# Fillers, the place of the ranking and the gather, and the last batch's first layer, in an mLSTM cell followed by a mixture of depths

## The chip, the core and the metric

The kernel runs on one core of a Trainium2 chip. The metric is the device time of one execution in microseconds, the median of several. Five engines work side by side, each through its own instructions in order: TensorE (PE; its weight loads are listed apart as PEld), VectorE (DVE), ScalarE (ACT), GpSimd (POOL) and SyncE (SP), which here only issues transfers. They wait for each other through semaphores. Matmul results go to PSUM[...]; everything else lies in SBUF.

## The reference

Two blocks follow one another. The first is an mLSTM cell over 4 batches, 8 heads, 768 steps and head dimension 40:

```python
for t in range(S):
    m_new = np.maximum(f_gate[:, :, t] + m, i_gate[:, :, t])
    f_stab = np.exp(f_gate[:, :, t] + m - m_new)
    i_stab = np.exp(i_gate[:, :, t] - m_new)
    m = m_new
    C = f_stab[..., None, None] * C + i_stab[..., None, None] * np.einsum('bhd,bhe->bhde', vt, kt)
    n = f_stab[..., None] * n + i_stab[..., None] * kt
    h_tilde = np.einsum('bhde,bhe->bhd', C, qt)
    denom = np.maximum(np.abs(np.einsum('bhd,bhd->bh', n, qt)[:, :, None]), 1.0)
    y[:, :, t] = sigmoid(o_gate[:, :, t]) * h_tilde / denom
```

Its output, seen as x of shape (4, 768, 320), goes to a mixture of depths:

```python
scores = np.einsum('bsd,d->bs', x, w_gate)
out = x.copy()
for b in range(B):
    top_idx = np.argpartition(-scores[b], capacity)[:capacity]   # capacity 128
    xe = x[b, top_idx]
    ye = np.maximum(xe @ w1, 0.0) @ w2                           # 320 -> 1024 -> 320
    out[b, top_idx] = x[b, top_idx] + sigmoid(scores[b, top_idx])[:, None] * ye
```

## The kernel before

Each batch of 768 rows is cut into six chunks of 128, so there are 24 steps n, with b = n // 6 and c = n % 6. Within a chunk the recurrence is a masked product: W is exp of a difference of two gate sums, one 128 x 128 block for each head, made by matmuls of prepared "operands" (a_o and M_o) into PSUM (pW) and an exp on ScalarE; GpSimd zeroes its upper part (`causal`). T holds k and q transposed, pS the products of k and q, P the product of pS and W, pH the chunk's own numerator and denominator. What comes from earlier chunks is the state C, decayed on GpSimd (`decay`) and enlarged by a product of k and wv, where wv is v scaled by `cols`; `exchange` makes both products in pIC.

```python
def warm(n):
    pw = ps_c.tile([128, 4 * L], FP, name="pw", tag="c")
    for _ in range(n):
        nc.tensor.matmul(pw, fill[:, 0:128], fill, start=True, stop=True)
...
def columns(g):                     # chunks 3g to 3g + 2: three transposes
    pc = ps_m.tile([128, 3, NR], FP, name="pc", tag="m")
    for j, row in enumerate((wk[g], r[g], r[g][:, L - 1:L].to_broadcast([NR, L]))):
        nc.tensor.transpose(pc[:, j, :], row, ident[0:NR, 0:NR])
    return pc

def keep(g, pc):                    # and their copy to SBUF
    both = const.tile([128, 3, NR], FP, name=f"cols{g}")
    nc.vector.tensor_copy(out=both, in_=pc)
...
def turned(n):                      # T[n]: four transposes and a copy, for k and for q
    T[n] = work.tile([128, 2, NP, L], FP, name="T")
    for j in range(2):
        turn(loaded[n][0], j, T[n])
```

Once a batch's six chunks are there, its rows are ranked by comparing every score with every other: `spread` puts a chunk's scores along the free dimension (sb), `compare` counts (ge, cnt), `columns_of` sums the counts over the chunks in PSUM (pcol), `ranked` turns them into ranks and one-hot selections. `number` makes row numbers of these by matmuls (pidx), and `gather` fetches the 128 rows from what has been stored, by an indirect transfer that GpSimd issues. The two layers of batch b are then spread over the steps of batch b + 1. The middle of a step, with the parts of the one-time steps 7 and 8 (NT is 6):

```python
pH = within(P[n], v1)
if n == NT + 1:
    pcol = columns_of(state[0][1][2])
elif n == NT + 2:
    picked[0] = gather(0, number(sel[0], token))
elif n == NT + 3:
    enter(0)
soon = c == 0 or n == N - 1
if n + 1 < N:
    decay(*steps[n + 1])
    hide(n + 1)                                    # causal, if not done yet
    give = exchange(*steps[n + 1], loaded[n + 1][0], T[n + 1], wv[n + 1])
    if n + 1 not in pS:
        pS[n + 1] = products(T[n + 1])
...
num, sor = norm(nums.get(n), pH, so)
if n + 1 < N:
    nums[n + 1] = exchanged(*steps[n + 1], *give)
    if n + 1 not in P:
        P[n + 1] = weighted(pS[n + 1], W[n + 1])
...
if n == NT + 1:
    ranked(0, pcol)
if n + 2 < N:
    stated(n + 2)                                  # wv
...
if c > 0:
    result(b, c, num, sor)                         # x, and its store
score(b, c, state[b][0])
```

The last batch has no steps after it, so its selection, its two layers and the scatter of its rows stand at the end. Its selected rows are made on chip, by matmuls of x and the selection (pX), already transposed; the last 64 of the 320 features fill only half the partitions, and the rest is zeroed:

```python
w = HW[-1][1]                                      # 64
if w < 128:
    nc.gpsimd.memset(last.xeT[w:, NDC - 1], 0.0)
...
for j, (d0, w) in enumerate(HW):
    for t in range(NT):
        nc.tensor.matmul(pX[j][0:w], x_t[b, t][:, d0:d0 + w], sel[:, t], start=(t == 0), stop=(t == NT - 1))
    if j < 2:
        copies[j](out=last.xeT[0:w, j], in_=pX[j][0:w])
...
copies[2](out=last.xeT[0:w, 2], in_=pX[2][0:w])
last.idx, last.xe = gather(b, number(sel_h, token))
last.first(0, NFC)                                 # 24 matmuls of 128x128x128, two copies with relu
last.gate()
last.gated()
last.second(0, NFC)                                # 8 matmuls of 128x128x320
last.leave()                                       # ye, and the scatter
```

The profile counts each float32 matmul as two, so `first` is 48 records and `second` 16.

Of the kernel before, what the change touches and what calls it, by code (L numbers as in the profile page):

```python
# [21 lines left out]
def kernel(  # L22
# [40 lines left out]
    assert S == NT * L and NT == 6 and D < DP and H == 8 and B == 4 and NFC == 8 and F_ == NFC * 128  # L63
# [27 lines left out]
    fill = const.tile([128, 4 * L], BF, name="fill")  # L91
# [91 lines left out]
    def warm(n):  # L183

        pw = ps_c.tile([128, 4 * L], FP, name="pw", tag="c")
        for _ in range(n):
            nc.tensor.matmul(pw, fill[:, 0:128], fill, start=True, stop=True)  # L187
# [108 lines left out]
    def load_w1(j):  # L296
        d0, w = HW[j]
        nc.sync.dma_start(out=w1[0:w, j, :], in_=moe_w1[d0:d0 + w, :])
# [204 lines left out]
    class Layers:  # L503
# [34 lines left out]

        def second(self, f0, f1):
            if f0 == 0:  # L540
                self.py = ps_m.tile([K_, DM], FP, name="py", tag="m")
            for f in range(f0, f1):
                nc.tensor.matmul(self.py, self.hT[:, f, :], w2[:, f, :], start=(f == 0), stop=(f == NFC - 1))  # L543
# [62 lines left out]
    def hide(n):  # L606
        if n not in hidden:
            causal(W[n])
            hidden.add(n)

    def run(hooks):
        for f in hooks:
            f()

    def step(n, **more):
# [5 lines left out]
        if n == NT + 1:  # L621
            pcol = columns_of(state[0][1][2])
        elif n == NT + 2:
            picked[0] = gather(0, number(sel[0], token))
        elif n == NT + 3:
            enter(0)

        soon = c == 0 or n == N - 1
        if n + 1 < N:
            decay(*steps[n + 1])  # L630
            hide(n + 1)
            give = exchange(*steps[n + 1], loaded[n + 1][0], T[n + 1], wv[n + 1])
# [16 lines left out]
        if n == NT + 1:  # L649
            ranked(0, pcol)  # L650
# [3 lines left out]
        if n < NT + 3:  # L654

            turned(n + 2)
            run(more.get("spread", ()))
# [22 lines left out]
        if c > 0:  # L680
            result(b, c, num, sor)
# [21 lines left out]
    warm(9)  # L703
# [7 lines left out]
    pW = masked([(ps_h, "h"), (ps_c, "c")])  # L711
    split(0, 0, nc.vector, slice(0, BH))
# [59 lines left out]
    turned(3)  # L772
    pH = within(P[1], loaded[1][1])
# [25 lines left out]
    step(2, places=[second_places], spread=[lambda: spread(0, *state[0][1][:2])],  # L799
         end=[lambda: compare(0, *state[0][1])])  # L800
    for n in range(3, N):
# [18 lines left out]
        if n == NT + 1 and HW[-1][1] < 128:  # L820
            nc.gpsimd.memset(w1[HW[-1][1]:, NDC - 1, :], 0.0)
# [34 lines left out]
    w = HW[-1][1]  # L856
    if w < 128:
        nc.gpsimd.memset(last.xeT[w:, NDC - 1], 0.0)
# [3 lines left out]
    pX = [(ps_s, "s"), (ps_s, "s"), (ps_t, "t")]  # L862
    pX = [pool.tile([128, K_], FP, name=f"pX{j}", tag=tag) for j, (pool, tag) in enumerate(pX)]
    for j, (d0, w) in enumerate(HW):
        for t in range(NT):
            nc.tensor.matmul(pX[j][0:w], x_t[b, t][:, d0:d0 + w], sel[:, t], start=(t == 0), stop=(t == NT - 1))
        if j < 2:
            copies[j](out=last.xeT[0:w, j], in_=pX[j][0:w])
# [36 lines left out]
```

## Time and profile before

| what | value |
|---|---|
| device time, median of 3 | 187.53 us (187.52 to 190.49) |
| device time of the profiled execution | 193.54 us |
| its span, first to last instruction | 191.8 us |
| PE, PEld, DVE, ACT, POOL busy | 179.0, 149.8, 139.8, 99.9, 101.4 us |
| transfers | 24.37 MB, 127 GB/s on average |
| costliest group on POOL | the masks of W, 46 of 718 ns, 32.0 us |
| costliest group on DVE | P, 48 of 685 ns, 30.9 us |
| costliest groups on PE | pS 29.7, pt 28.2, pH 28.1, ph 23.8 us |

The page of a profile gives for each group of instructions its line, engine, operation, the tiles it writes and reads, how many there are and how long one takes, and then the idle time of the engine just before them and what ended most of it. The chain follows the execution back from its last instruction, at each step to what released it. The timeline lists instructions by start; a bracket at its end is the idle time before, with the releaser. "(x319)" is a number of instructions. Matmuls overlap, so a busy PE need not be PE at its peak.

### The profile page before, as it was taken

The numbers are of one execution on the slowest core, as the hardware profiler recorded it, in microseconds if no ns is written. First come the engines' busy times: TensorE is split into PE (matmuls) and PEld (weight loads), VectorE is DVE, ScalarE is ACT, GpSimd is POOL, SyncE is SP. The second block draws the span as 40 slices with busy tenths as digits, with TensorE's granted clock in tenths as the row PEclk, the third lists the DMA queues.
The fourth block names the chain that finished last, engine by engine and source line by source line (L and its number), as shares of the span: only waits on it lengthen the run. The fifth ranks groups of instructions, "written<-read, shape, count | busy, mean of one in ns | idle before, by whom it ended". The sixth has DMA issues, their size and how long they took to land.

```text
span 191.8 us, 6510 instructions
## 1 busy us (share of the span) xinstructions
PE 179.0 (93%) x2594; PEld 149.8 (78%) x2594; DVE 139.8 (73%) x413; ACT 99.9 (52%) x233; POOL 101.4 (53%) x171
## 2 busy tenths in 40 slices
PE   6999999789999887999999999999999999989990
PEld 2577888677877775989878889798788898859960
DVE  7633748988999868867899778868997788585101
ACT  3054466589898678466734473567344734201110
POOL 7954356597676639413774657327746571023202
PEclk9999999999999999999999999999999999999999
DMA  4999996597998999999999498597993101010100
GB/s 79 140 156 148 145 171 100 108 173 151 198 223 180 164 224 251 170 172 183 159 172 143 98 166 152 104 188 120 147 127 83 39 34 38 36 38 36 34 0 34
DMA packets 105854, 24.37 MB, mean 127 GB/s; under 512 B 100640, under 2 KB 105248, under 8 KB 105824
## 3 DMA queue, kind: packets, MB, share of 16 engines
q1 hardware_dynamic: 105008, 22.50, 74.0%
q0 software_dynamic: 384, 1.31, 2.2%
q8 instruction: 20, 0.33, 0.8%
q10 hardware_dynamic: 432, 0.15, 0.7%
q14 instruction: 10, 0.08, 0.2%
HBM read 19.37 MB, written 4.59 MB: 125 GB/s over the span
## 4 chain that ended last, share of the span: by engine, by line
PE 65%; issue 11%; DVE 11%; POOL 7%; DMA 3%; ACT 1%; POOLq 1%; ACTq 0%
PE pS L363 11%; PE pH L420 10%; PE pt L308 10%; PE ph L534 9%; PE py L543 5%; PE pIC L389 4%; PE pIC L395 4%; PE pW L341 3%; DVE P L369 3%; POOL W L347 3%; PE pw L187 2%; DMA out_dram<-ye,idx 2%; DMA xe<-out_dram,idx 2%; DVE ge L459 1%; POOL sor L435 1%
## 5 line engine op out<-in xcount | busy, mean ns | idle before, releaser
L342 ACT ACTIVATE W<-pW 128x512 f32<-128x512 f32 x48 | 26.1, 595 | 24.6 <-PE pW L341 15.2
L435 POOL TENSOR_TENSOR sor<-so,rec 128x320 f32<-128x320 f32 x24 | 17.8, 740 | 39.1 <-DVE rec L433 32.8
L347 POOL TENSOR_SCALAR_AFFINE_SELECT W<-W 128x512 f32<-128x512 f32 x46 | 32.0, 718 | 10.9 <-ACT W L342 10.9
L369 DVE TENSOR_TENSOR P<-pS,W 128x512 f32<-128x512 f32 x48 | 30.9, 685 | 7.6 <-PE pS L363 3.7
L309 ACT COPY T<-pt 128x512 f32<-128x512 f32 x47 | 25.5, 589 | 20.0 <-PE pt L308 19.7
L420 PEld LDWEIGHTS pH<-v,P 128*64 128x64 f32 x768 | 24.9, 140 | 9.8 <-DVE x L440 5.5
L420 PE MATMUL pH<-v,P 128*64 128x64 f32 x768 | 28.1, 227 | 3.8 <-DVE x L440 2.4
L363 PE MATMUL pS<-T 64*128 64x128 f32 x384 | 29.7, 297 | 0.0
L308 PE MATMUL pt<-ident,qk 128*128 128x128 f32 x192 | 28.2, 294 | 0.0
L363 PEld LDWEIGHTS pS<-T 64*128 64x128 f32 x384 | 24.9, 199 | 2.5 <-issue 1.3
L459 DVE SCALAR_TENSOR_TENSOR ge<-sb,sc,earlier 128x128 bf16<-128x128 f32 (+5 forms) x23 | 17.5, 764 | 11.0 <-ACT sb L453 10.9
L308 PEld LDWEIGHTS pt<-ident,qk 128*128 128x128 f32 x192 | 23.3, 151 | 1.5 <-issue 0.2
L534 PE MATMUL ph<-xeT,w 128*128 128x128 f32 x192 | 23.8, 280 | 0.0
L534 PEld LDWEIGHTS ph<-xeT,w 128*128 128x128 f32 x192 | 22.1, 192 | 1.7 <-issue 1.6
L543 PE MATMUL py<-w,hT 128*128 128x320 f32 x64 | 19.3, 442 | 0.0
L354 POOL TENSOR_TENSOR wv<-v,cols 128x328 f32<-128x328 f32 x20 | 15.1, 756 | 5.4 <-DVE cols L284 5.4
L446 DVE CUSTOM_DVE_ANT_0 scr<-x,wg 128x320 f32<-128x320 f32 x24 | 15.7, 652 | 0.7
L543 PEld LDWEIGHTS py<-w,hT 128*128 128x128 f32 x64 | 11.5, 191 | 5.0 <-issue 1.4
L389 PE MATMUL pIC<-C,T 128*64 128x82 f32 x320 | 15.2, 236 | 0.0
L549 POOL DMA_INDIRECT out_dram<-ye,idx x4 | 4.6, 1144 | 19.4 <-DVE ye L547 19.4
L395 PE MATMUL pIC<-wv,qk 128*64 128x41 f32 x320 | 12.8, 230 | 0.7 <-POOL wv L354 0.7
L377 POOL TENSOR_TENSOR C<-C,cols 128x328 f32<-128x328 f32 x16 | 13.0, 810 | 0.2
(150 smaller groups left out, 265.4 us busy)
## 6 DMA issues: line engine op xcount, KB each, us to landing
qk<-in_k_dram SPq DMA_DIRECT2D x24, 160.0 KB, 4.4
qk<-in_q_dram SPq DMA_DIRECT2D x24, 160.0 KB, 4.8
v<-in_v_dram SPq DMA_DIRECT2D x24, 160.0 KB, 5.0
so<-in_o_gate_dram SPq DMA_DIRECT2D x24, 160.0 KB, 4.4
out_dram<-x SPq DMA_DIRECT2D x24, 160.0 KB, 2.0
w<-in_moe_w_dram SPq DMA_DIRECT2D x2, 640.0 KB, 5.8
w<-in_moe_w_dram SPq DMA_DIRECT2D x2, 512.0 KB, 4.6
w<-in_moe_w_dram SPq DMA_DIRECT2D x1, 256.0 KB
```

The source lines that it names most:

```text
L308: nc.tensor.transpose(pt[:, p, :], qk[:, j, 2 * p:2 * p + 2, :].rearrange("s a d -> s (a d)"), ident)
L309: copy(out=T[:, j], in_=pt)
L342: nc.scalar.activation(out=W[:, h0:h0 + 4, :], in_=pW, func=AF.Exp)
L347: nc.gpsimd.affine_select(out=W[:, h0:h0 + 4, :], in_=W[:, h0:h0 + 4, :], compare_op=OP.is_ge, fill=0.0, base=0, pattern=[[0, 4], [1, L]], ...
L363: nc.tensor.matmul(pS[j][:, p, :], T[e, 0, p, :], T[e, 1, p, :], start=True, stop=True)
L369: nc.vector.tensor_tensor(out=P[:, :, j, :], in0=pS[j], op=OP.mult, in1=W.rearrange("p (n a) t -> p n a t", a=2)[:, :, j, :])
L389: nc.tensor.matmul(pI[t, 2 * p * D1:2 * (p + 1) * D1], T[:, 1, p, t], C[:, p].rearrange("e a d -> e (a d)"), start=True, stop=True)
L395: nc.tensor.matmul(pC[e, p, :], qk[:, 0, 2 * p + j, :], wv[:, 2 * p + j, :], start=True, stop=True)
L420: nc.tensor.matmul(pH[t, 2 * p + j, :], P[:, p, j, t], v1[:, 2 * p + j, :], start=True, stop=True)
L435: nc.gpsimd.tensor_tensor(out=sor, in0=so, in1=rec.unsqueeze(2).to_broadcast([128, H, D]), op=OP.mult)
L534: nc.tensor.matmul(self.ph[:, f % 4, :], w1[:, j, f * 128:(f + 1) * 128], self.xeT[:, j, :], start=(j == 0), stop=(j == NDC - 1))
L543: nc.tensor.matmul(self.py, self.hT[:, f, :], w2[:, f, :], start=(f == 0), stop=(f == NFC - 1))
```

## The change

It has five parts.

- The fillers at the start, matmuls that only keep TensorE busy while the gates load, read one column of ones, broadcast, instead of a block of 512 columns that has to be filled first. There are ten ahead of the first real matmuls for nine, and one more behind the matmuls of the mask of chunk 0.
- The transposes and the copy that make `cols` for chunks 3 to 5 move from step 2's neighbourhood to step 1's, and the transposes of chunk 4's k and q move ahead of chunk 1's result. The first score's `spread` moves up with them.
- At step 7 chunk 7's result x is written before the first batch is ranked.
- At step 8 the row numbers are made where they were, but the gather is issued behind the decay and the mask of step 9. The memset that zeroed the unused 64 rows of w1's last part is gone: these rows are now loaded with a second copy of the 64 rows of weights. In the layers of batches 0 to 2 they meet zeros, as before.
- In the tail the last 64 features of the selected rows are made twice, in the lower and the upper half of the partitions. With the weights in both halves too, the products of these 64 features alternate between the halves of the array, each over 64 partitions instead of 128 that are half zeros. They are done first, for all eight blocks of the hidden layer, in eight PSUM banks; then the other 256 features are added, and each block gets its relu by itself, on ScalarE and VectorE by turns. The memset of xeT is gone.

```diff
-    fill = const.tile([128, 4 * L], BF, name="fill")
+    fill = const.tile([128, 1], BF, name="fill")
     nc.vector.memset(fill, 1.0)
 ...
-        pw = ps_c.tile([128, 4 * L], FP, name="pw", tag="c")
+        pw = ps_s.tile([128, 4 * L], FP, name="pw", tag="s")
         for _ in range(n):
-            nc.tensor.matmul(pw, fill[:, 0:128], fill, start=True, stop=True)
+            nc.tensor.matmul(pw, fill.to_broadcast([128, 128]), fill.to_broadcast([128, 4 * L]), start=True, stop=True)
 ...
         d0, w = HW[j]
-        nc.sync.dma_start(out=w1[0:w, j, :], in_=moe_w1[d0:d0 + w, :])
+        for p in range(0, 128, w):
+            nc.sync.dma_start(out=w1[p:p + w, j, :], in_=moe_w1[d0:d0 + w, :])
 ...
+        def first_at_once(self, banks):
+            ph = [pool.tile([128, K_], FP, name="ph", tag=tag) for pool, tag in banks]
+            for f, p in enumerate(ph):
+                e = HALVES[f % 2]
+                nc.tensor.matmul(p, w1[e, NDC - 1, f * 128:(f + 1) * 128], self.xeT[e, NDC - 1], start=True, stop=False)
+            for f, p in enumerate(ph):
+                for j in range(NDC - 1):
+                    nc.tensor.matmul(p, w1[:, j, f * 128:(f + 1) * 128], self.xeT[:, j, :], start=False,
+                                     stop=(j == NDC - 2))
+                if f % 2:
+                    nc.vector.tensor_scalar(out=self.hT[:, f, :], in0=p, scalar1=0.0, scalar2=None, op0=OP.max)
+                else:
+                    nc.scalar.activation(out=self.hT[:, f, :], in_=p, func=AF.Relu)
 ...
         elif n == NT + 2:
-            picked[0] = gather(0, number(sel[0], token))
+            pidx = number(sel[0], token)
 ...
             decay(*steps[n + 1])
             hide(n + 1)
+            if n == NT + 2:
+                picked[0] = gather(0, pidx)
             give = exchange(*steps[n + 1], loaded[n + 1][0], T[n + 1], wv[n + 1])
 ...
+        if n == 2:
+            spread(0, *state[0][1][:2])
 ...
         if n == NT + 1:
+            result(b, c, num, sor)
             ranked(0, pcol)
 ...
-            turned(n + 2)
-            run(more.get("spread", ()))
+            if n + 2 not in T:
+                turned(n + 2)
 ...
-        if c > 0:
+        if c > 0 and n != NT + 1:
             result(b, c, num, sor)
 ...
-    warm(9)
+    warm(10)
 ...
     pW = masked([(ps_h, "h"), (ps_c, "c")])
+    warm(1)
     split(0, 0, nc.vector, slice(0, BH))
 ...
     turned(3)
+    keep(1, columns(1))
     pH = within(P[1], loaded[1][1])
 ...
     run(operands(0, 4, [(ps_m, "m")]))
+    stated(3)
+    turned(4)
     result(0, 1, num, sor)
     nums[2] = exchanged(0, 2, *give)
-    keep(1, columns(1))
-    stated(3)
 ...
-        if n == NT + 1 and HW[-1][1] < 128:
-            nc.gpsimd.memset(w1[HW[-1][1]:, NDC - 1, :], 0.0)
 ...
-    w = HW[-1][1]
-    if w < 128:
-        nc.gpsimd.memset(last.xeT[w:, NDC - 1], 0.0)
 ...
-    pX = [(ps_s, "s"), (ps_s, "s"), (ps_t, "t")]
+    pX = [(ps_s, "s"), (ps_s, "s"), (ps_t, "t"), (ps_t, "t")]
     pX = [pool.tile([128, K_], FP, name=f"pX{j}", tag=tag) for j, (pool, tag) in enumerate(pX)]
+    to = [[(pX[0], slice(0, 128))], [(pX[1], slice(0, 128))], [(pX[2], HALVES[0]), (pX[3], HALVES[1])]]
     for j, (d0, w) in enumerate(HW):
         for t in range(NT):
-            nc.tensor.matmul(pX[j][0:w], x_t[b, t][:, d0:d0 + w], sel[:, t], start=(t == 0), stop=(t == NT - 1))
+            for p, e in to[j]:
+                nc.tensor.matmul(p[e], x_t[b, t][:, d0:d0 + w], sel[:, t], start=(t == 0), stop=(t == NT - 1))
 ...
-    copies[2](out=last.xeT[0:w, 2], in_=pX[2][0:w])
+    nc.scalar.copy(out=last.xeT[HALVES[1], 2], in_=pX[3][HALVES[1]])
+    nc.vector.tensor_copy(out=last.xeT[HALVES[0], 2], in_=pX[2][HALVES[0]])
     last.idx, last.xe = gather(b, number(sel_h, token))
-    last.first(0, NFC)
+    last.first_at_once([(ps_s, "s"), (ps_s, "s"), (ps_t, "t"), (ps_t, "t"), (ps_h, "h"), (ps_c, "c"), (ps_m, "m"),
+                        (ps_m, "m")])
```

More of the change, by code (lines that the diff above doesn't have):

```diff
@@ L61 @@
     AHEAD = 4
-    assert S == NT * L and NT == 6 and D < DP and H == 8 and B == 4 and NFC == 8 and F_ == NFC * 128
+    assert HW[-1][1] == 64 and S == NT * L and NT == 6 and D < DP and H == 8 and B == 4 and NFC == 8 and F_ == NFC * 128
     assert 0 < capacity <= 128
@@ L798 @@
     gated(3)
-    step(2, places=[second_places], spread=[lambda: spread(0, *state[0][1][:2])],
+    step(2, places=[second_places],
          end=[lambda: compare(0, *state[0][1])])
@@ L861 @@
     copies = (nc.scalar.copy, nc.scalar.copy, nc.vector.tensor_copy)
-    pX = [(ps_s, "s"), (ps_s, "s"), (ps_t, "t")]
+    pX = [(ps_s, "s"), (ps_s, "s"), (ps_t, "t"), (ps_t, "t")]
     pX = [pool.tile([128, K_], FP, name=f"pX{j}", tag=tag) for j, (pool, tag) in enumerate(pX)]
+    to = [[(pX[0], slice(0, 128))], [(pX[1], slice(0, 128))], [(pX[2], HALVES[0]), (pX[3], HALVES[1])]]
     for j, (d0, w) in enumerate(HW):
         for t in range(NT):
-            nc.tensor.matmul(pX[j][0:w], x_t[b, t][:, d0:d0 + w], sel[:, t], start=(t == 0), stop=(t == NT - 1))
+            for p, e in to[j]:
+                nc.tensor.matmul(p[e], x_t[b, t][:, d0:d0 + w], sel[:, t], start=(t == 0), stop=(t == NT - 1))
         if j < 2:
-            copies[j](out=last.xeT[0:w, j], in_=pX[j][0:w])
+            copies[j](out=last.xeT[:, j], in_=pX[j])
     own.leave()
```

## The prediction

> **What bounds the kernel now.** I read the run times first, then the chain in order of time, the table by stages, and the timelines of the three places that the change touches. Chunks are numbered n = 0 to 23, batch by batch. The profiled execution took 193.54 us, the median of the plain runs is 187.53; the chain says where the difference may lie:
>
> ```profile
> 7.92 1.90 PE pt L308 x8
> ...
> 21.48 1.90 PE pt L308 x8
> ...
> 27.96 1.04 PE pt L308 x8
> ...
> 59.15 0.87 PE pt L308 x8
> ```
>
> Columns: start, us, what. The same eight transposes take 1.90 us until 21.48 and 1.04 or 0.87 afterwards: TensorE ran at about half speed until some 24 us. Its pieces of the chain from 6.93 to 24.95 sum to 17.6 us; at the later rates (pt 0.87 to 1.04, pS 1.09 for 2.01, pH 1.08 for 1.56, pIC 0.45 for 1.01, pO 0.44 for 0.75) they would be about 9. So the 6 us between the profile and the median can be this stretch, and I take a plain run to be at full speed much earlier. The rest of the kernel by stages:
>
> ```profile
> 25.00:35.00 10.00, 9.32 (x181) 7.92 (x181) 7.52 (x21) 7.58 (x19) 6.16 (x10) 1.00 0.78 114
> 35.00:55.00 20.00, 18.16 (x329) 15.38 (x326) 18.39 (x57) 16.33 (x41) 15.28 (x30) 1.00 0.98 187
> 55.00:75.00 20.00, 17.30 (x321) 14.04 (x318) 16.82 (x47) 16.13 (x42) 13.31 (x18) 1.00 1.06 184
> 75.00:100.00 25.00, 24.97 (x386) 21.94 (x387) 20.64 (x57) 14.66 (x35) 12.79 (x19) 1.00 1.06 179
> ```
>
> Columns: stretch, length, then PE, PEld, DVE, ACT, POOL busy, clock, DMA share, GB/s. From 75 us to 165 PE is busy all the time (24.97 of 25): there only less PE work helps, and the change brings none. From 35 to 75 PE has gaps and VectorE carries the chain. A microsecond won before 75 us should reach the end, because PE then starts its solid part earlier. Three stretches have gaps that the change aims at. First, chunk 3's operands:
>
> ```profile
> 35.13 0.46 DVE L284 COPY cols<-pc 128x288 f32<-128x288 f32 x1
> 35.67 1.04 POOL L354 TENSOR_TENSOR wv<-v,cols 128x328 f32<-128x328 f32 x1 [1.64 <-DVE cols L284]
> 36.76 0.67 PE L395 MATMUL pIC<-wv,qk 128*64 128x41 f32 x16 [0.73 <-POOL wv L354]
> 39.78 1.15 PE L420 MATMUL pH<-v,P 128*64 128x64 f32 x32
> ```
>
> The bracket is idle time before, and its releaser: copy, then wv, then PE, each waiting for the one before. Second, the first gather:
>
> ```profile
> 67.64 0.48 DVE L440 TENSOR_TENSOR x<-pH,sor 128x320 f32<-128x320 f32 x1
> 68.17 1.15 PE L420 MATMUL pH<-v,P 128*64 128x64 f32 x32 [0.87 <-DVE x L440]
> 70.05 1.23 POOL L498 DMA_INDIRECT xe<-out_dram,idx  x1 [4.03 <-DVE idx L496]
> 71.35 0.73 POOL L377 TENSOR_TENSOR C<-C,cols 128x328 f32<-128x328 f32 x1
> 72.04 1.21 POOL L347 TENSOR_SCALAR_AFFINE_SELECT W<-W 128x512 f32<-128x512 f32 x2
> 73.29 1.29 DVE L369 TENSOR_TENSOR P<-pS,W 128x512 f32<-128x512 f32 x2 [0.52 <-POOL W L347]
> 74.49 0.48 DVE L440 TENSOR_TENSOR x<-pH,sor 128x320 f32<-128x320 f32 x1
> 75.03 1.15 PE L420 MATMUL pH<-v,P 128*64 128x64 f32 x32 [1.09 <-DVE x L440]
> ```
>
> GpSimd stands 4.03 us in front of the gather, while decay and mask behind it were ready. Third, the tail:
>
> ```profile
> 177.09 5.44 PEld L534 LDWEIGHTS ph<-xeT,w 128*128 128x128 f32 x48
> 177.12 5.60 PE L534 MATMUL ph<-xeT,w 128*128 128x128 f32 x48
> 182.56 4.47 PE L543 MATMUL py<-w,hT 128*128 128x320 f32 x16
> 187.07 0.55 DVE L547 SCALAR_TENSOR_TENSOR ye<-py,g,xe 128x320 f32<-128x320 f32 x1 [3.24 <-PE py L543]
> ```
>
> First layer, second layer, result, one after the other to the end.
>
> [...] the 16 half-height pS matmuls take 1.09 us, 68 ns each, the full ones of the first layer 5.60/48 = 117. [...] Two masks took 1.22 us mostly, but 1.55 and 1.80 beside compares at 61.38 and 55.99[...].
>
> **The change part by part**, in the profile's times.
>
> *Fillers.* The memset of fill took 0.48 us (0.99 to 1.47) and held back the first filler until 1.53. With one column it is near 0.06 (as the 128x1 memset of twos at 3.42), so PE starts at about 1.1. Nine fillers took 4.02, so 10 take some 4.45 and end at 5.55 as before: at half speed nothing is lost or gained. VectorE gets to its first scan up to 0.4 sooner, but it began at 3.74 and the third f_sb load, issued at about 1.7 with a median of 1.7 to landing, comes at some 3.4: 0.3 at most. The filler after the masks' matmuls (end 6.93) costs 0.43 at half speed before pm, nothing at full. I put 0.2 gained. The unbroken stretch grows from about 1.5 to 6.9 into 1.1 to 7.4, so the clock is caught more surely: half a microsecond on average for a plain run, and I hold this number loosely.
>
> *Chunk 3's operands.* The 0.46 us copy and the three transposes (0.48 us of PE at 33.11) leave n = 2 for n = 1. Then wv need not wait: it can run right after the select that ends at 34.03, so PE's pIC no longer stands 0.73. The transposes of chunk 4 (0.87 to 1.0) fill the gap of 0.65 before pH. On VectorE score, add and reciprocal move up by 0.46, and the second score, 0.90 beside wv and decay, may be 0.49: together 0.9 sooner for x and so for pH at 39.78. But at n = 1 PE carries the chain in the profile, and the three transposes delay chunk 3's W by about 0.4 there. Net 0.6.
>
> *x ahead of ranking.* At n = 7 rank, rank and sel (66.37 to 67.6) stood before x. Now x goes from 66.46 to 66.94, and pH waits for something else: pO needs the bank of pcol, which the second rank operation frees 0.48 later than now, at 67.2; pO and pW then end at 67.8. So pH(8) starts at 67.8, not 68.17: 0.4.
>
> *Gather behind the decay.* GpSimd now does the decay at 65.1 to 65.9, the mask when W comes (ACT at about 67.9, so 68.5 to 69.7), then the gather at 69.8 to 71.0, then sor. The mask is gone from VectorE's way; P(9) now waits for pS, num and C. VectorE: idx 69.3, add, reciprocals to 70.6, num and C to 71.9 (in the profile num began only at 71.52, for a reason I can't read; if that stays, 0.6 later), P to 73.2, x to 73.7. So pH(9) starts at 73.7 to 74.3, not at 75.03: 0.7 to 1.3, the 0.4 above in it. I take 1.1. The gather takes 4.7 us to land at this load: 74.5, and PE wants it after pH(9) at 74.9, just in time. The memset of w1's rows (0.95 us at 65.08) ran while GpSimd was idle anyway: nothing. The second load of 64 rows is 256 KB, some 1.4 us of transfers at 184 GB/s; the operands for n + 4 are asked for two steps, over 10 us, before use and land after 4.4 to 6.8: hidden.
>
> *Tail.* The last third of the first layer, 16 of 48 matmuls at 117 ns = 1.87, becomes 16 half-height ones at 68 = 1.09: 0.78 won. Twelve more pX matmuls are 64 columns wide and alternate between halves; pH's 32 such ones take 1.15, 36 ns each for half the columns, so overlapping I expect the same 1.4 us for 24 as now for 12. But these products now come first, and wait for the copies of pX (282 ns after 177.06) which the full ones hid: start about 177.4, not 177.1: 0.3 lost. Eight copies of 128 columns on two engines replace two of 512; each ends under its successor's 0.47 us. Net 0.5.
>
> Sum: 0.2 + 0.6 + 1.1 + 0.5, and 0.5 for the clock = 2.9, so 187.5 - 2.9 = 184.6 us.
>
> **Rivals.** (a) The start is bound by loads: five chunks of 640 KB at the 148 GB/s of 8 to 25 us need 22 us, so a plain run already waits for data there, and an earlier clock and earlier operands give nothing. For it: DMA share 1.33 in that stretch; against: no engine's wait before 35 us names a load. Then 185.5 to 186. (b) The clock is the main thing: if plain runs still spend 3 to 7 us at half speed and the longer fillers end that, 1.5 to 3 us more, 182 to 183. For it: the runs' spread up to 190.49; against: two runs at 187.52 and 187.53. (c) The new order makes a wait of its own: the gather lands after 75 us and PE stands at n = 9, or the half-width products don't overlap (24 x 117 = 2.8 us for 1.4). Then 186 to 187.5.
>
> **Range and chances.** The parts that rest on visible gaps give 2 to 3 us; (a) and (c) take up to 2 off, (b) adds up to 3. So 182.0 to 187.3. Faster by over 2% needs under 183.78, which takes part of (b): 0.36. Within 2% 0.60; slower by over 2% needs a fault that I see no sign of: 0.04.
>
> **What would show it.** Right, if GpSimd's wait before the first gather falls from 4.03 to under 1 us and the mask precedes it; pH at n = 9 has no wait for x of over 0.7; pIC at n = 2 doesn't wait for wv; the stage from 25 us on keeps its PE rates; first layer 4.8 us from its first matmul, starting some 0.3 after pX. Wrong, if pX at n = 9 waits for the gather, pX's last third takes over 2 us, or eight transposes still take 1.9 us after 10 us.

## The result, and the profile after

The changed kernel takes **189.87 us** (median of 4 runs, 189.55 to 190.11), the kernel before 187.53: a ratio of **1.0132**, 95% interval 1.0106 to 1.0158. The prediction was 184.6 us, range 182.0 to 187.3. It was wrong, and in direction. Medians here and below are over all executions of a kernel, while the ratios leave out disturbed executions of both, so the two need not agree to the last digit. The 2.3 us between the medians is rough: beside the experiments below, 165 more executions of the kernel before have a median of 189.3 us. That the changed kernel is the slower one rests on the ratio; a second run gave 1.0119 (0.9997 to 1.0242).

The profile of before in the prediction was an execution of 193.54 us in which eight transposes still took 1.97 us at 21.42 in PE's timeline. A second profile of the same kernel, 187.56 us, has them at 1.09 us from 7.38 on and is used from here on ("before"). The first place to look is the stage table; columns are stretch, length, then PE, PEld, DVE, ACT, POOL busy, clock, DMA share, GB/s. After:

```profile
35.00:55.00 20.00, 19.27 (x336) 15.52 (x334) 18.63 (x50) 17.37 (x44) 14.28 (x25) 1.00 1.07 192
55.00:75.00 20.00, 16.54 (x274) 13.97 (x270) 13.54 (x42) 12.09 (x31) 9.63 (x13) 0.83 0.97 203
75.00:100.00 25.00, 25.00 (x407) 22.44 (x405) 20.43 (x57) 13.95 (x31) 12.09 (x17) 1.00 1.16 165
```

Before, the middle one of these stages:

```profile
55.00:75.00 20.00, 16.34 (x294) 13.94 (x291) 15.30 (x45) 13.37 (x33) 11.74 (x16) 1.00 1.02 195
```

Of the stages of after only the one from 55 to 75 us has a clock below 1.00, and TensorE gets through 20 instructions fewer in it than before. The timeline of PE in it (start, us, what, and in brackets the idle time before with its releaser):

```profile
65.81 1.15 PE L422 MATMUL pH<-v,P 128*64 128x64 f32 x32
69.64 0.87 PE L516 MATMUL pX<-ident,xe 128*128 128x128 f32 x3 [2.67 <-DMA xe<-out_dram,idx]
70.44 1.36 PE L391 MATMUL pIC<-C,T 128*64 128x82 f32 x16
71.59 1.03 PE L397 MATMUL pIC<-wv,qk 128*64 128x41 f32 x16
72.55 2.08 PE L365 MATMUL pS<-T 64*128 64x128 f32 x16
74.56 0.59 PE L343 MATMUL pW<-M_o,a_o 32*128 32x512 bf16 x2
```

pH(9) starts at 65.81, in before at 67.93: the change has won 2.1 us by here. Then PE stands 2.67 us for the gathered rows, and afterwards everything takes nearly twice as long. In before the same place reads:

```profile
70.18 0.52 PE L514 MATMUL pX<-ident,xe 128*128 128x128 f32 x3 [1.10 <-ACT so L320]
70.63 0.79 PE L389 MATMUL pIC<-C,T 128*64 128x82 f32 x16
71.25 0.61 PE L395 MATMUL pIC<-wv,qk 128*64 128x41 f32 x16
```

(The releaser named, a copy on ScalarE, had long been done; the gather landed at 70.0.) The rows came at nearly the same moment in both kernels, at 70.0 before and 69.5 after. The stage table cut into microseconds (columns: stretch, length, PE busy, clock, DMA share, GB/s) shows the clock of after:

```profile
67.00:68.00 1.00, 0.00 (x0) 1.00 1.18 233
68.00:69.00 1.00, 0.00 (x0) 0.60 0.82 114
69.00:70.00 1.00, 0.36 (x2) 0.50 1.05 156
...
74.00:75.00 1.00, 1.00 (x8) 0.50 1.24 278
75.00:76.00 1.00, 1.00 (x10) 0.99 1.50 147
```

The clock falls 1.2 us after PE stops, and full speed comes back only at 75.0, although PE is busy from 69.64 on; the clock reads 0.50 in between.

A ledger of one profiled execution each shows where the time goes. Its rows are differences between starts of pH(n), the matmuls that open a step (us). "Filled" and "repaired" are the experiments `both_filled` and `enter_fill` below.

| stretch | before | after | filled | repaired |
|---|---|---|---|---|
| start to pH(0) | 16.45 | 16.66 | 16.43 | 16.36 |
| pH(0) to pH(3): chunk 3's operands | 16.23 | 15.75 | 16.17 | 15.99 |
| pH(3) to pH(7) | 21.26 | 21.33 | 21.33 | 21.33 |
| pH(7) to pH(8): x ahead of ranking | 7.13 | 6.38 | 6.38 | 6.37 |
| pH(8) to pH(9): gather behind decay and mask | 6.86 | 5.69 | 5.69 | 5.74 |
| pH(9) to pH(10): the gathered rows | 8.46 | 12.46 | 9.68 | 8.36 |
| pH(10) to the end of the span | 109.41 | 109.33 | 109.32 | 109.55 |
| span | 185.8 | 187.6 | 185.0 | 183.7 |

After against before: -1.9 in steps 7 and 8, -0.5 at chunk 3, +0.2 at the start, +4.0 at step 9; together +1.8 us of span. The remaining 0.5 us or so of the 2.34 between the medians lies outside the span (see "The start and the time outside the span").

### The profile page after: what moved, and what is told of

Its sections match the earlier page's. It is cut to its first block, busy times and chain, and to the rows that moved or that the text cites. A ratio compares the mean times of both kernels' runs of the same rounds, so it can differ in the third digit from the quotient of the medians.

```text
span 187.6 us, 6543 instructions
## 1 busy us (share of the span) xinstructions
PE 173.8 (93%) x2608; PEld 145.5 (78%) x2608; DVE 140.1 (75%) x417; ACT 100.1 (53%) x236; POOL 99.8 (53%) x169
## 4 chain that ended last, share of the span: by engine, by line
PE 54%; DMA 12%; DVE 11%; SPq 9%; issue 9%; POOL 3%; POOLq 1%; ACT 0%; ACTq 0%; DVEq 0%
PE pS L365 10%; PE ph L536 9%; PE pH L422 9%; SPq L121 9%; PE pt L310 7%; DMA xe<-out_dram,idx 5%; PE py L560 5%; PE pIC L391 5%; PE pIC L397 3%; PE pW L343 3%; DMA v<-in_v_dram 3%; DVE P L371 2%; DMA wg<-in_moe_w_gate_dram 2%; DVE ge L461 2%; DVE scr L448 2%
## 5 line engine op out<-in xcount | busy, mean ns | idle before, releaser
L365 PE MATMUL pS<-T 64*128 64x128 f32 x384 | 28.8, 291 | 0.0
L461 DVE SCALAR_TENSOR_TENSOR ge<-sb,sc,earlier 128x128 bf16<-128x128 f32 (+5 forms) x23 | 18.0, 784 | 11.5 <-ACT sb L455 11.5
L365 PEld LDWEIGHTS pS<-T 64*128 64x128 f32 x384 | 24.1, 193 | 2.0 <-issue 0.7
L310 PE MATMUL pt<-ident,qk 128*128 128x128 f32 x192 | 25.5, 276 | 0.0
L310 PEld LDWEIGHTS pt<-ident,qk 128*128 128x128 f32 x192 | 21.2, 141 | 1.4
L536 PE MATMUL ph<-xeT,w 128*128 128x128 f32 x144 | 18.2, 281 | 0.0
L536 PEld LDWEIGHTS ph<-xeT,w 128*128 128x128 f32 x144 | 16.7, 192 | 1.9 <-issue 1.8
L391 PE MATMUL pIC<-C,T 128*64 128x82 f32 x320 | 15.8, 241 | 0.0
L391 PEld LDWEIGHTS pIC<-C,T 128*64 128x64 f32 x320 | 13.2, 141 | 0.6 <-issue 0.3
```

What stands on the lines that cost most here:

```text
L310: nc.tensor.transpose(pt[:, p, :], qk[:, j, 2 * p:2 * p + 2, :].rearrange("s a d -> s (a d)"), ident)
L365: nc.tensor.matmul(pS[j][:, p, :], T[e, 0, p, :], T[e, 1, p, :], start=True, stop=True)
L391: nc.tensor.matmul(pI[t, 2 * p * D1:2 * (p + 1) * D1], T[:, 1, p, t], C[:, p].rearrange("e a d -> e (a d)"), start=True, stop=True)
L461: nc.vector.scalar_tensor_tensor(out=ge[:, GE[u]:GE[u + 1]], in0=sb.rearrange("p t l -> p (t l)")[:, 0:n], scalar=sc[:, u:u + 1], in1=earl ...
L536: nc.tensor.matmul(self.ph[:, f % 4, :], w1[:, j, f * 128:(f + 1) * 128], self.xeT[:, j, :], start=(j == 0), stop=(j == NDC - 1))
```

## The experiments

My theory after the result: the landing of the gather is set by the transfers, so time won upstream became a wait at step 9, and this longer wait cost the clock. Rivals: the place of the gather on GpSimd is at fault; other parts of the change lose the time; the wait alone is the loss and the clock follows other causes. Each of these groups ran side by side on a chip of its own: `before_again`, `fill_wait`, `gather_first`, `w2_later`; `after_again`, `enter_later`, `enter_fill`, `enter_turn`; `best_again`, `tail_old`, `order_old`, `cols_old`; `both_filled`, `before_enter`, `enter_w2`; `start_six`, `turn_one`, `turn_two`. Across groups only ratios and differences of over half a microsecond are used; the kernel before has medians of 188.6 to 190.0 us in them.

**Wait or clock.** First the kernel before in a more typical execution, then three versions of the changed kernel. `fill_wait` puts eleven fillers ahead of the transposes that wait, `both_filled` also eight at the start of step 3, where PE stands 1.7 us; `enter_later` moves the transposes behind work that is ready.

> The kernel before, unchanged, for a profile of an execution near its median. If the first 24 us at half speed are what set the earlier profile apart, this one takes about 187.5 us, its eight transposes fall to about 1.1 us before 12 us, and PE does not stand for the first gather: it lands before PE wants it. If the kernel before also stands for its first gather in such an execution, the loss of the changed kernel is not there.

187.56 us, clock 0.994. This is the profile used above.

```diff
         elif n == NT + 3:
+            warm(11)                # fill_wait
             enter(0)
```

> The changed kernel with 11 filler matmuls (some 2.4 us at full speed) ahead of the transposes that wait for the first gather, at step 9. They keep TensorE busy and shorten no wait. If the half clock after the wait is a loss of its own, the pieces from 69.6 to 75 us fall back to their full rates and the time is 2.2 to 2.8 us lower, 187.1 to 187.7 us. If the wait alone is what costs, the time stays at 189.5 to 190.2 us.

187.18 us (186.48 to 188.02, 20 runs), ratio 0.9959 (0.9932 to 0.9986). The rows land hardly sooner (69.2 for 69.5), but PE keeps its clock (0.998 on average in its profiled execution, 0.982 in after), and the loss against the kernel before is gone.

```diff
         load(n + AHEAD)
+        if n == 3:
+            warm(8)                 # both_filled: this and the eleven of fill_wait
         pH = within(P[n], v1)
```

> The changed kernel with nothing moved: eight fillers at the start of step 3 and eleven at step 9 ahead of the transposes that wait for the gather. TensorE still has to wait for the rows, but stays at full clock in both places. If the loss is the clock (half rate costs about 2.6 us at step 9 and 1 to 1.5 at step 3 where it happens): 186.4 to 186.9, tight. If the wait itself is most of it: 188 or more. What is left above 185.5 is the wait's own price.

186.68 us (186.52 to 187.12, 6 runs), ratio 0.9889 (0.9839 to 0.9939), as the clock theory had it. The timeline of PE at step 9:

```profile
67.31 2.35 PE L187 MATMUL pw<-fill 128*128 128x512 bf16 x10 [0.16 <-issue]
69.50 0.49 PE L516 MATMUL pX<-ident,xe 128*128 128x128 f32 x3
69.92 0.79 PE L391 MATMUL pIC<-C,T 128*64 128x82 f32 x16
70.54 0.61 PE L397 MATMUL pIC<-wv,qk 128*64 128x41 f32 x16
```

pX starts at 69.50, in after at 69.64: about the same wait, filled, though here the rows landed at 68.6 and the fillers themselves held the last 0.9 us. pIC takes 0.79 for 1.36, and from pX to pH(10) it is 6.18 us, not 8.63. So the clock costs 2.45 us. `fill_wait`, where the rows landed at 69.2 and pX starts at 69.42, says the same (6.21 us to pH(10)), and so do the median spans, 187.45 in after and 185.0 here. The other 1.65 of the 12.46 - 8.36 = 4.1 us between after and repaired at step 9 is the wait itself.

```diff
-        elif n == NT + 3:
-            enter(0)
 ...
             hide(n + 2)
+            if n == NT + 3:
+                enter(0)            # enter_later
             layer(b, c)
```

> The changed kernel; only the three transposes that wait for the first gather stand later in step 9, behind the products and the W of the next steps, just ahead of the layer that needs them. Theory A (PE stands 2.7 us for the gather and loses 2.6 us at half clock): PE works through the wait, pX has to wait under 0.5 us, and the time is 184.6 to 185.6 us. Rival, the gather only shifts the wait: the layer's matmuls or the next steps wait instead, 187 us or more.

186.32 us (185.42 to 190.52, 17 runs), ratio 0.9906 (0.9876 to 0.9936). PE no longer stands for the rows. Its profiled execution shows a drop elsewhere, at the hole that opened in step 3 when the transposes of chunk 4 moved up:

```profile
32.30 1.30 PE L422 MATMUL pH<-v,P 128*64 128x64 f32 x32 [1.72 <-issue]
33.33 1.37 PE L391 MATMUL pIC<-C,T 128*64 128x82 f32 x16
34.43 1.09 PE L397 MATMUL pIC<-wv,qk 128*64 128x41 f32 x16
```

From pH(3) to pH(4) it takes 6.87 us; after has the same hole, 1.74 us at 32.41, kept its clock there in its profiled execution, and takes 5.93. `enter_fill` is `enter_later` with the eight fillers of step 3; `best_again` is its second run.

> As enter_later, and 8 fillers (1.75 us at full speed) at the start of step 3, where PE now has nothing from about 30.65 to 32.41 us because the transposes of chunk 4, which were there, have moved up. If this hole costs the clock in some executions (one profile shows pIC, pS at half rate from 33 to 37 us), the spread of the times shrinks and the median is 0.3 to 1 us under enter_later's. If the hole is harmless, the two are equal within 0.2 us.

**185.46 us** (185.30 to 185.58, 6 runs), ratio **0.9879** (0.9818 to 0.994), beside `enter_later`. This version beats both kernels.

```profile
30.50 1.92 PE L187 MATMUL pw<-fill 128*128 128x512 bf16 x8
32.35 1.15 PE L422 MATMUL pH<-v,P 128*64 128x64 f32 x32
...
69.45 0.55 PE L516 MATMUL pX<-ident,xe 128*128 128x128 f32 x3
70.96 2.27 PE L536 MATMUL ph<-xeT,w 128*128 128x128 f32 x18 [0.96 <-ACT xeT L518]
```

pH(3) runs at full rate behind the fillers. pX starts when after's did, but now without a wait of note: two pIC groups, pS and W(11) lie before it. The first layer waits 0.96 us for the copies instead, still far less.

> The changed kernel with batch 0's transposes of its gathered rows behind W(11) in step 9 and eight fillers at the start of step 3, run a second time as the base of the three runs beside it. If its first result (ratio 0.988 to the kernel before) was no accident of one chip, it repeats at 0.985 to 0.991, about 185.4 us.

185.67 us (185.42 to 186.32, 6 runs), ratio 0.9849 (0.9803 to 0.9894): it holds.

> The changed kernel, unchanged, many executions beside the kernel before on this chip. If PE's wait for the first gather and the half clock behind it are what every execution pays, the time stays near 189.9 us and the mean clock near 0.98. If the half clock depends on [...], some executions keep the clock, and they are 2.2 to 2.8 us lower, at about 187.2 us, as the version with fillers in the wait is.

The unchanged after once more, beside `enter_later`: 191.87 us (188.95 to 193.57, 6 runs), ratio 1.0119 (0.9997 to 1.0242). In its profiled execution the wait is 2.58 us, the half rate lasts from 69.0 to 79.2, and from pX to pH(10) it is 10.59 us: 4.4 more than in `both_filled`.

**Does the gain belong to the repair?** `before_enter` is the kernel before with its transposes of the gathered rows moved in the same way.

> The kernel before with only the transposes of batch 0's gathered rows moved behind W(11). In the profile before its PE waits 1.1 us there. If the repaired kernel's gain is the change's own: at most 0.5 us under the kernel before, ratio 0.995 to 1.0. If moving those transposes alone makes most of the repaired kernel's gain: ratio under 0.992.

187.9 us (187.31 to 194.56, 22 runs), ratio 0.9953 (0.9923 to 0.9982). pH(9) to pH(10) is 8.36 for 8.46, so the repair alone is worth 0.1 us there while the clock holds. In plain runs it is worth more: the kernel before, unchanged beside it, has a median of 190.0 us and mean clocks down to 0.957, this one 187.9 and none under 0.988, and the ratio allows a gain of up to 1.4 us. The kernel before thus loses its clock in many executions too; where, no profile shows. The change's own gain, once the wait is gone, is best read beside this run, from `enter_w2` below, which has the change, the repair and the fillers: 185.47 us, or 2.4 less.

**What sets the landing.**

```diff
         elif n == NT + 2:
-            pidx = number(sel[0], token)
+            picked[0] = gather(0, number(sel[0], token))     # gather_first
```

> The changed kernel with the first gather back in front of the decay and the mask, nothing else. Theory B, order: the gather goes out early enough, PE does not stand for it, 184.6 to 186 us. Theory A, traffic: the gather's row numbers exist only at 61.9 us, so it goes out at 62.2 instead of 62.6 and meets the same transfers; it lands 0.4 us sooner at best, and the mask comes 1 us later: 189.3 to 190.5 us.

189.35 us (185.53 to 192.6, 20 runs), ratio 0.9993 (0.9948 to 1.0039). The expectation got no clear answer from the times. The profiled run was its fastest: gather issued at 62.20, w2 behind it, landed 5.9 us later, no wait and no drop (the clock reads 1.00 from 64 to 74 us). Most of its executions are slower, with mean clocks of 0.961 to 0.986; where they lose it was not traced. That the place of the gather on GpSimd makes the loss is refuted by `enter_fill`, where it stands behind decay and mask and the loss is gone.

```diff
-        elif 3 + NDC <= n < 5 + NDC:
-            load_w2(n - 3 - NDC)
+        elif 6 + NDC <= n < 8 + NDC:
+            load_w2(n - 6 - NDC)    # w2_later; in enter_w2 on top of enter_fill
```

> The changed kernel with the two loads of w2 three steps later (after steps 9 and 10), nothing else. Theory A, traffic: the first half of w2 (640 KB) is issued 0.16 us ahead of the first gather, which so lands after 6.9 us; PE stands 2.7 us for it and then runs some 5 us at half clock, 2.6 us more. Then here the gather lands after 4 to 5 us, PE stands under 0.7 us, no half clock follows, and the time is 184.6 to 185.6 us. Theory B, order: the gather is late because it now stands behind the decay and the mask on GpSimd. Then this changes nothing: 189.5 to 190.2 us.

187.53 us (184.78 to 188.19, 4 runs). Landing 5.8 us after issue, PE's wait 1.53, no drop at step 9 (pIC takes 0.79 us behind the wait), but one at the hole of step 3 (1.36 behind 1.83 us). The time lies between the two forecasts: the transfer ahead does matter, but only for about 1 of the 6.9 us.

> The repaired kernel (transposes of the gathered rows behind W(11), eight fillers at step 3) with both w2 loads three steps later, so that 640 KB less stand ahead of the gather. If transfers set the landing: it lands 5.8 to 6.0 us after its issue and not 6.9, and the first layer at step 9 starts up to 0.5 us sooner; time 185.0 to 185.4. If the landing is set by the issue alone: as the repaired kernel, 185.4 to 185.8, or slower if the later loads collide with step 12's operands.

185.47 us (185.25 to 185.59, 6 runs), ratio 0.982 (0.9771 to 0.987). The gather lands 5.4 us after its issue, and the first layer starts at 70.89 for 70.96: no gain, since W(11) and the copies stand before it anyway. It was half right: the transfer ahead does delay the landing, but with the transposes moved it doesn't matter.

Set beside each other, the landings sort by where the 640 KB half of w2 stands. In before:

```profile
61.08 0.42 SPq L302 DMA_DIRECT2D w<-in_moe_w_dram  x1
62.94 1.23 POOL L498 DMA_INDIRECT xe<-out_dram,idx  x1 [4.03 <-DVE idx L496]
```

In after, with the landing (us from issue, at the end of the line):

```profile
62.45 0.43 SPq L304 DMA_DIRECT2D w<-in_moe_w_dram  x1
xe<-out_dram,idx POOLq DMA_INDIRECT x1, 6.9
```

It is issued ahead of the gather in before (61.08 and 62.94), after (62.45 and 62.61) and `enter_fill` (62.03 and 62.55): 7.1, 6.9 and 6.9 us, and in the twelve other profiled executions with w2 ahead it is 6.6 to 7.6. It is issued behind it in `gather_first` (62.96) and `both_filled` (63.05 after 62.80): 5.9 and 5.8. With the load moved away, in `w2_later` and `enter_w2`: 5.8 and 5.4. The profile that the prediction read had w2 at 65.04, 5.0 us ahead of the gather: 4.7 us.

**The parts by themselves**, each undone in `enter_fill` and run beside `best_again` (185.67 us).

`order_old` has x behind the ranking and the gather ahead of decay and mask, as before:

```diff
-            pidx = number(sel[0], token)
+            picked[0] = gather(0, number(sel[0], token))
 ...
-            if n == NT + 2:
-                picked[0] = gather(0, pidx)
 ...
         if n == NT + 1:
-            result(b, c, num, sor)
             ranked(0, pcol)
 ...
-        if c > 0 and n != NT + 1:
+        if c > 0:
```

> The same kernel with chunk 7's result behind the ranking and the gather ahead of decay and mask, as in the kernel before. If these two parts really win some 2.1 us at steps 7 and 8 and the end sees it once nothing waits for the gather: 1 to 2 us slower than the base. If the start of the gather alone counts, since the transfers set its landing: no slower, and its order was of no worth.

187.54 us (187.33 to 188.45, 22 runs), ratio 0.9931 (0.9904 to 0.9958): **1.9 us slower** than the base. One thing I had not expected: in its profiled execution the clock drops without any wait above 0.9 us:

```profile
59.80 0.34 PE L244 MATMUL pO<-a,placea 32*128 32x128 bf16 x3 [0.58 <-DVE rank L482]
...
61.19 1.81 PE L422 MATMUL pH<-v,P 128*64 128x64 f32 x32 [0.87 <-DVE x L442]
62.94 0.32 PE L493 MATMUL pidx<-token,sel 128*128 128x1 f16 x6
63.18 1.36 PE L391 MATMUL pIC<-C,T 128*64 128x82 f32 x16
```

Here there are two holes, 0.58 and 0.87 us, with half a microsecond of work between them. That execution took 188.45; most of its others 187.3 to 187.9.

`tail_old` has the tail of before (64 features once, the rest zeroed, two banks), with the second 64 rows of w1 still loaded:

```diff
+    nc.gpsimd.memset(last.xeT[w:, NDC - 1], 0.0)
 ...
-    last.first_at_once([(ps_s, "s"), (ps_s, "s"), (ps_t, "t"), (ps_t, "t"), (ps_h, "h"), (ps_c, "c"), (ps_m, "m"),
-                        (ps_m, "m")])
+    last.first(0, NFC)
```

> The same kernel with the tail of the kernel before: 64 features once, the rest zeroed, two banks of four blocks. The prediction's tail (0.5 us): 0.5 us slower than the base beside it. From the profile after (sel to ye 14.68 us for 14.79): 0.1 us slower, so the difference hardly shows.

185.83 us (185.54 to 186.07, 6 runs), ratio 0.9847 (0.9803 to 0.9891): 0.16 us slower than the base with overlapping ranges, so the half-height tail is worth some 0.1 to 0.2 us.

`cols_old` has no fillers at step 3 and chunk 3's operands, chunk 4's transposes and the first spread in their old places:

```diff
-        if n == 3:
-            warm(8)
 ...
     turned(3)
-    keep(1, columns(1))
 ...
-    stated(3)
-    turned(4)
     result(0, 1, num, sor)
     nums[2] = exchanged(0, 2, *give)
+    keep(1, columns(1))
+    stated(3)
```

> The same kernel without the fillers of step 3, and with chunk 3's operands, chunk 4's transposes and the first spread in their old places. By the prediction's step (0.6 us for this part): 0.6 us slower than the base. By the profile after (steps 2 to 3 won 0.5, of which a hole of 1.7 us on TensorE follows): within 0.3 us of the base, in either direction, with no hole and so no need of fillers.

186.46 us (185.89 to 187.2, 6 runs), ratio 0.989 (0.9843 to 0.9938): 0.8 us slower, but the median spans are 184.25 and 183.9, so 0.35 us of it lies in the kernel's work and the rest outside the span.

`enter_turn` is `enter_later` with only the transposes of chunk 4 in their old place:

```diff
     stated(3)
-    turned(4)
     result(0, 1, num, sor)
```

> As enter_later, and the transposes of chunk 4 back where they were before the change. If moving them up won time, this is slower than enter_later by up to 0.5 us. If it only made the hole at 30.65 us, this equals enter_fill: 0.3 to 1 us faster in the median than enter_later.

186.08 us (185.52 to 186.73, 16 runs), ratio 0.9909 (0.9883 to 0.9936), beside `enter_fill`. Median spans 183.65 and 183.75: moving the transposes up won nothing. It widened the hole in front of pH(3), 0.87 us here, to the 1.7 us that fillers then had to close.

**The start and the time outside the span.** Device time minus span is 1.7 to 1.8 us in all executions of before and `before_enter`, and 1.7 to 1.9 in `fill_wait`, `both_filled`, `enter_fill`, `best_again`, `tail_old`, `order_old` and `enter_w2`, which all have eight or more fillers behind the start. It is 2.0 to 2.6 in after, and mostly 2.0 to 3.05 in `after_again`, `w2_later`, `gather_first`, `enter_turn` and `cols_old`, which have the new start and no such fillers; `enter_later`, without them too, has 1.7 to 1.9 in eight of 17 executions and 2.4 to 2.7 in nine. To find the reason, `enter_turn` was given other numbers of fillers: six at the start for ten; one at the start of each of steps 4 to 7; two there.

```diff
-    warm(10)
+    warm(6)                         # start_six
```
```diff
         load(n + AHEAD)
+        if 4 <= n < 8:
+            warm(2)                 # turn_two; warm(1) in turn_one
```

> The version with the gathered rows' transposes behind W(11) and chunk 4's transposes in their old place (enter_turn: span 183.7 us, device time 2.3 to 2.8 us above the span), with six fillers at the start for ten: 2604 matmuls for 2608. If the number of TensorE's instructions decides on the time outside the span: device time 1.7 us above the span as in the kernel before. If fillers behind the start decide it: still 2.5. The clock may be caught later for lack of fillers, which lengthens the span alone.

191.68 us (188.85 to 194.6, 4 runs); outside the span 2.9 in three and 1.85 in one. The number of TensorE's matmuls alone is thus not it: `tail_old` has the same 2604 and 1.7. What it shows of the start is more useful. The timeline of PE,

```profile
0.99 2.74 PE L187 MATMUL pw<-fill 128*128 128x512 bf16 x6 [0.99 <-DVE fill L92]
4.88 0.45 PE L201 MATMUL pe<-FM,ident 96*32 96x2 f32 x6 [1.15 <-POOL a L227]
...
13.67 1.95 PE L310 MATMUL pt<-ident,qk 128*128 128x128 f32 x8
...
20.18 1.15 PE L422 MATMUL pH<-v,P 128*64 128x64 f32 x32
```

has one hole of 1.15 us behind the fillers; the eight transposes still take 1.95 us at 13.67, and pH(0) comes at 20.18 for 16.36 in `enter_turn`.

> The same with one filler at the start of each of steps 4 to 7: 2612 matmuls. If the number of instructions decides by where it ends: 1.7 or 2.5, and it shows how near to 2608 the change lies. If fillers as such decide: 1.7.

187.03 us (186.19 to 187.87, 20 runs), ratio 0.9945 (0.9919 to 0.9971); outside the span 1.9 to 3.35, median 2.55.

> The same version with two fillers at the start of each of steps 4 to 7, 2616 matmuls for 2608, as many as the version with eight fillers at step 3, where no hole needs them. If the number of TensorE's instructions or any fillers behind the start decide on the time outside the span: 1.7 us. If it is only the filled hole of step 3 that does: 2.5. The span itself: 183.7, or up to 1 us more where the fillers stand in PE's way.

187.09 us (186.68 to 188.87, 20 runs), ratio 0.9966 (0.9939 to 0.9994); outside the span 1.7 to 1.9 in all twenty, while the span is 1.65 us longer because the fillers stand in PE's way. Eight added fillers, not a filled hole, go with the shorter time outside the span; four do not, and without any it comes out either way. By which means is open: nothing in a trace lies there.

## Why the prediction was wrong, point by point

**The step that failed** is the landing: "The gather takes 4.7 us to land at this load: 74.5, and PE wants it after pH(9) at 74.9, just in time." It was the one row at hand, from an execution in which the w2 load was 5.0 us ahead; in executions nearer the median, with w2 0.16 to 1.9 us ahead, it is 6.9 (after) to 7.1 (before). With 6.9 the same working gives 69.8 + 6.9 = 76.7, a wait of 1.8 us; the other 0.9 of the 2.67 goes with the gain upstream, which was larger than predicted (1.9 for 1.1). From before to after the issue moved by 0.3 us (62.94 to 62.61) and PE's need by 2.1. A margin of 0.4 us on a transfer of 4.7 was none. The prediction named this wait as a sign of being wrong, but gave it no cost in its sum.

**Rival (c)** named this wait and bounded it at 186 to 187.5 us. That bound was too low, because it counted the wait only: the wait cost 1.65 us, the clock 2.45 more. The prediction reckoned with the half rate at the start alone and gave a wait no price in clock. Here 2.67 us in after and 1.72 in `enter_later` were followed by a clock of 0.50. Why the prediction's own profile stayed at half rate is open: PE is busy for all 16.00 us from 8 to 24 in it, and the eight transposes at 21.42 still take 1.97.

Two readings of the prediction are off, with nothing resting on them: the pieces of the chain from 6.93 to 24.95 sum to 18.0 us, not 17.6; and the mask at 61.38 ran beside a score, for the most part, not a compare.

The terms of the sum (2.9 us), from the ledger and the runs with a part undone:

- *Fillers, 0.2 predicted:* nothing. pH(0) starts at 16.33 to 16.71 in versions with this start, at 16.45 in before.
- *Clock at the start, 0.5 on average:* nothing in the median, since the execution of before near the median had the clock already (1.09 us for eight transposes at 7.38, as in after at 7.59). The idea was right for the others: of 165 executions of before beside the experiments, 17 are at 193.4 us or more at a mean clock of 0.987 to 1.0, as the first profile; of 185 executions with the ten fillers, none is above 188.9 us at such a clock.
- *Chunk 3's operands, 0.6:* 0.35 between the median spans of `cols_old` and the base. wv no longer stands in PE's way, as predicted, and VectorE's copy is out of its chain at n = 2, but x of chunk 2 comes 15.42 us after pH(0) with the old order (`cols_old`) and 15.13 with the new (`best_again`): 0.3 of the 0.46 predicted, and pH(1) is 0.1 later. The 0.4 more that the second score was to give did not come: in after it takes 0.90 us as ever:

```profile
28.25 0.49 DVE L448 CUSTOM_DVE_ANT_0 scr<-x,wg 128x320 f32<-128x320 f32 x1
...
28.78 0.90 DVE L448 CUSTOM_DVE_ANT_0 scr<-x,wg 128x320 f32<-128x320 f32 x1
```

- *x ahead of ranking, 0.4, and gather behind the decay, 0.7:* right in mechanism, too small: 0.75 and 1.17, together the 1.9 us of `order_old`. `gather_first`, which undoes the second alone, has 6.83 us from pH(8) to pH(9) for 5.69, so 1.14. GpSimd in after:

```profile
60.97 1.37 POOL L349 TENSOR_SCALAR_AFFINE_SELECT W<-W 128x512 f32<-128x512 f32 x2 [2.28 <-ACT W L344]
62.61 1.23 POOL L500 DMA_INDIRECT xe<-out_dram,idx  x1 [0.27 <-DVE den L431]
```

  The 4.03 us in front of the gather are 0.27, the mask precedes it, and pH(9) has no wait for x.
- *Tail, 0.5:* 0.1. Columns as in the other timelines; after:

```profile
173.41 1.16 PE L546 MATMUL ph<-xeT,w 64*128 64x128 f32 x16 [0.23 <-DVE idx L498]
174.50 3.84 PE L549 MATMUL ph<-xeT,w 128*128 128x128 f32 x32
...
178.26 4.57 PE L560 MATMUL py<-w,hT 128*128 128x320 f32 x16
...
182.87 0.55 DVE L564 SCALAR_TENSOR_TENSOR ye<-py,g,xe 128x320 f32<-128x320 f32 x1 [3.17 <-PE py L560]
```

  The rates are as predicted (1.09 us for the half-height products, 4.85 for the layer), and pX's 48 matmuls take 4.41 us for 4.40 of 36. But the layer to be replaced took 5.45 from start to start, not 5.60, so it won 0.60; it starts 4.87 us after pX's first matmul for 4.49, which loses 0.38, and from py to ye it is 4.61 for 4.51, which loses 0.10.

So the change by itself is worth 0.35 + 1.9 + 0.1 = 2.35 us where nothing waits for the gather, and `enter_w2` beside `before_enter` shows 2.4 on one chip; the prediction's 2.9 was not far. That a gain ahead of 75 us reaches the end held too: from pH(10) on it is 109.3 to 109.6 us in all four columns of the ledger. What was missing is the + 4.0 at step 9. Rival (a), a start bound by loads, is not refuted by these runs, but isn't needed: in the profile of before the only wait put down to a load ahead of 35 us is 0.3 us. Rival (b), half speed at the start of plain runs, did not come about in that profile (pH(0) at 16.45); the clock did matter, but at step 9 and as a loss.

## What to carry to other kernels

A time won ahead of a transfer is kept only if the transfer can move too: before counting it, ask when the first reader now wants the data, when the transfer lands among the others that are then under way, and what other ready work can be put before that reader. A hole on TensorE can cost the clock on top of its own length (2.67 us cost 2.45 more, 2.58 once 4.4), and a shorter one is not always safe (behind 1.72 us in `enter_later` the clock fell to 0.50), so put ready work or fillers into it (with fillers the clock stayed at 1.00 at step 9 of `both_filled`) rather than compare holes by length. Read durations for such sums from an execution that is like the median, not from the one that happens to be profiled.

## What the runs showed of the hardware that I had not expected

- **The half rate lasted one, two or three times 3.41 us in the four drops dated here.** Taken in stretches of 0.25 to 1 us, the clock column gives 61.43 to 64.85 in `order_old`, 33.15 to 36.57 in `enter_later`, 68.19 to 75.02 in after, 69.0 to 79.2 in `after_again`: 3.42, 3.42, 6.83 and 10.2. In the 3.41 us ahead of each of the first three drops PE was busy 1.6 to 2.2 us, as its timeline adds up. But from 29.74 to 33.15 in after it was busy 1.61 us, and the clock stayed at 1.00 there. Why a hole costs nothing in one execution (1.74 us at step 3 of after) and a microsecond in another (1.72 in `enter_later`) was not shown, nor why `after_again` stayed low for 10.2 us, although PE was busy from 69.64 on. The rows that date the first:

```profile
61.25:61.50 0.25, 0.25 (x8) 0.86 0.05 8
61.50:61.75 0.25, 0.25 (x12) 0.50 0.08 15
64.50:64.75 0.25, 0.25 (x12) 0.50 0.91 280
64.75:65.00 0.25, 0.25 (x12) 0.81 1.21 275
```

- **The clock column doesn't show the slow start.** In `start_six` it reads 1.00 while the transposes take 1.95 us, from 13.67 on (the same eight take 1.09 in `enter_turn`); there the durations must be read:

```profile
12.00:14.00 2.00, 2.00 (x18) 1.00 1.51 140
14.00:16.00 2.00, 2.00 (x12) 1.00 1.50 156
```

- **The 640 KB ahead of a gather cost it about 1 us** (6.6 to 7.6 in fifteen profiled executions against 5.4 to 5.9 in four), whether they are issued 1.9 or 0.2 us before it.
- **Some 0.75 us more of device time lies outside the span** in most executions with the new start, and is gone in every version with eight or more fillers behind the start, wherever they stand. That is a part of the changed kernel's loss that no reading of its trace could have found.
